# Attention and routed experts on one core: a new order table for attention's 2230 tasks

## Chip, core and metric

One Trainium2 chip, one of its cores. The metric is the device time of one execution in microseconds (us). The kernel's five instruction streams are TensorE (PE, the matrix engine, with its weight loads shown apart as PEld), VectorE (DVE), ScalarE (ACT), GpSimd (POOL) and SyncE (SP), which here issues nearly all DMAs.

## What is computed

Attention over 8 batches of 12 heads (448 positions, head size 64) with RMS-normalized q and k, and behind it a router with 8 experts, each of which takes exactly 448 of the 3584 tokens:

```python
q_n, k_n = (rmsnorm(q, g_q), rmsnorm(k, g_k))
scores = np.matmul(q_n, k_n.transpose(0, 1, 3, 2)) / np.sqrt(64)
scores = scores - np.max(scores, axis=-1, keepdims=True)
attn = np.exp(scores)
attn = attn / (np.sum(attn, axis=-1, keepdims=True) + 1e-09)
x = np.matmul(attn, v).transpose(0, 2, 1, 3).reshape(3584, 768)
logits = x @ w_gate                       # (3584, 8)
# all 3584*8 logits are gone through from the largest down; a token goes to
# expert e if it has none yet and e has fewer than 448 tokens
out[mask_e] = np.maximum(x[mask_e] @ w1[e], 0.0) @ w2[e]
```

## The kernel before

The kernel has two stages. In the first, some 405 us long, attention makes the rows x and the logits; then the router assigns tokens, and the experts gather their rows and multiply. The change lies in the first stage alone.

**Tiling.** The 96 heads are 24 groups of four (`g`), each two pairs of heads; there are 48 pairs. For a group, q and k are loaded by SP (`_load` L242 for the first 384 positions, `_tails` L249 for the last 64), squared and summed (DVE L320), normalized (POOL L353), split into a high and a low f16 part (ACT L388, POOL, DVE), and turned by DMA transposes from SP (L429). Then a first product on PE gives score maxima (`max_score` L539, DVE's `max_reduce` L550 reads them from the PSUM tiles `pm` and `psc`). The maxima of a group become one row of the second operand: ACT's `put_max` L555, PE's transposition (L485), ACT's copy `mt` (L489) and SP's two small DMAs `q<-mt` (`row_max`, L496). After that PE computes `scores` (L569, into `psc`), ACT exponentiates (`exp`, L580) and PE multiplies by the values (`av`, L604, f32, accumulated in the bank `po`; for part of the pairs the last 64 positions come apart, in 64-row matmuls, `av_tail`). DVE divides by the sum (`x_norm`, L639 to L643), ACT and DVE split x into f16 parts (`x_hi` L654 and L655, `x_lo` L660 and L661), PE transposes a part of it (`x_here`, L678, into the pair's own `po` bank), DVE copies it out (`x_here_out`, L371), DMAs turn the rest (L691) and store it (L700, L704), and PE multiplies by the gate's weights (`gate` L741 to L750; for the last batch `gate_last` L762 to L764). The logits of a batch come out as a sum (`gate_lo` on ACT, L783 and L784, then `gate_sum` on DVE, L789 and L790), of the last batch as a copy (`gate_copy`, L777 and L778).

**Buffers.** PSUM has two `psc` tiles, one `pm` tile and two `po` banks. The `po` banks carry the value products of a pair from its first `av` to its `x_here_out`, the gate's sums, and a few small things; so the value products of pair n+2 can't begin before pair n is done with. q and k have rings of two to three groups, the exponentials `e` one of nine tiles.

**Side work.** The router's constants are made in between: DVE casts the rank tables (`rankt`, `rankb`, both at L1143) and the second half of the gate's weights is made by `gate_weights` (L187).

**What sets the order.** `Attention.plan` lists 2230 tasks (763 on PE, 516 on DVE, 483 on ACT, 258 on SP, 210 on POOL), each with the tasks that it must follow. `Attention.ORDER`, a string of digit pairs in base 64, is a permutation of them. `Plan.run` (L84) decodes it and calls the tasks one after the other:

```python
order = [64 * digit[a] + digit[b] for a, b in zip(table[::2], table[1::2])]
assert all(a == b or at[a] < at[b] for a, b in self.edges())
for n in order:
    self.tasks[n][3](*self.tasks[n][4])
```

Each engine executes its own instructions strictly in this order; between engines only semaphores hold it. So the table sets, on each engine, which task stands behind which. How far one task stands behind another on PE is given below in PE's work between the two: the number of matmuls that stand there, by the start-to-start times of their kinds in the trace.

Of the kernel before, what the change touches and what calls it, by code (L numbers as in the profile page):

```python
# [89 lines left out]
class Attention:  # L90
# [926 lines left out]
    def plan_first(self, plan, g, a, t):  # L1017
# [42 lines left out]
                 port=False, frees=[("rf", *x)])  # L1060

    ORDER = (
        "020z0o01080706000509030+0-100A0p0q0r04111213141u1t1v1w1x1y2n2r2p2o0w2q2s0x0y3G3F0s0B151T161U1718191V1A1B1C1D"
        "1W1X1E1F1Y1Z1K1G1a1H1J1L1M1NCi1c1b1+1-1i1j1z2L1ICj1kCkCmCo2M20212N2O2P1l221d231O242Q1m2t1e251fCpClCn261h272R"
        "1P2v1Q1R2C1r281g2u2S1SCq29G+H02T2U2D2V2wG-2W2xH1Cr0C2ACsCuCw2ECtH2CxCv2y2a2b2z2+2B2-3H2G1nH32X2Y1o1q2F1pH43I"
        "CyH6Cz0t3J2Z3KH52cC+D0ME303132H73h3m3k493j3i1s3l4A2k3n33MKH8MGH93L3p3M343N3P3O35373QC-2dD1D2MJD3D42HHAMF2IHB"
        "2e2JD53q2KD6D8MH36D73oD9HC2jHDHEHFML3r4B0uDADB3RMIS44CS5S6MNHGMOMPHHS73s2f3T3S3U3t3u3v2l3E2m4b4g4f4c3V3W4d4e"
        "543X3w38DCMRMMDD2gS82iDE2hS9MQDFDHHIHKHJHL4DDGSASBDIDJDKHODLDMSCSD3D4E3x39MSHMMY3AMVMWMUMXHNSE3B3CHP4h3z4j4F"
        "4G3y3+4H4I4J533e3-40410vSFSGDNSHDODPMZMaDQMbMTHQDSDRSISJSKHSHRHTMdDTMcHUDVDUHWDWSLSMDXHVHXHYHZ3ZSNMfMeSORU3a"
        "HaMgMjMmMlMh4L3bHbSPSQ4iSR4kSSST4M4KDYHcMiMkSUDZDaDb3Y3d554lHd4m574N5V3c4O5+4P5X5Y3f0D4n4p4o5W4RSV4q3g4Q485a"  # L1070
        "5z5Z56RVMnHeMoDdDcHgSWSXSYHfHhSZDeDfSaDgMqMpHiMrMtSbDhMsHjScDiHkRW4344Hl0E0F450GSdSeSfSgSh58MuHmHnMxHoMwMzHq"
        "MvSu4r4s42HpHrDj46SmSl4vSvDkDlRXN0MyDmN2N4M+DoHsHuN1DnSwSxSy595b4t5A4u475B5D5CHtHv4x5EDpDrSzM-S+Dq5cHwN3HyN5"
        "HxHzS-DsT0H+5dH-Dt4TRYI0I24UN8N9NB5FT1T2T3T4T5I14VI3Sn4w5eT6T75-4X5H5f5g61DuDvDw5G4S5I5h5i4ySj4Y6P6u4W6U5J6R"
        "4Z6Q5K4aNANCRZDxNFN6NGNEDyDzD+NHN7I4E06ST8T90HD-62TAI6NISk6t6T525L5j5kI5I7I8I9E1E2IANJNDTBICIB4zIDTCTFTGTHTI"
        "4+TDIEIF4-IGTE0ITJSoSqTKSp60TLE3Sr50IH636451Ss5l6V5n6XE4StE5Si655m5o665pNKNLNONNNQRaE6NMNPIIE86768IKIJILNWNR"
        "IM6WTMTNTOE7TPTQIONSINIP6YTRE9TSEANVNXNTNUEBRbECTTTUTVED6Z696a6v6xIQIRTWISNYNZNb5r6b6A5M5q5S7J7O7n5NIT5O5PIU"
        "IV6B5R6c6C6d5Q6yTXTkTlEE6wEFEGRcNgNkNcNeEHNiNaIWEJEINdTmTnToIYIXIZTd7o7K7L6DTp6f6g6F6e5s5T6E7N7M5U5yEKEMNfNj"
        "IaIcNhIbIdIeIfELTqTrTsENEONlIgRd5t5uIh5v6zTtTuTvTwTxNoIiNpNsNmNqIj0J6h7P6+7R5x6i6-70TyTzEPEQERReNxNnES5wNzIk"
        "NvEUETImNrT+T-U0IlIoInIpU173EVEWEXU2NuNyIqNwEYIsIrIt6jTbTcNtEZU3IuU5U6U7U46H6k71746l726G6IIwTeTfTgU86J7QU9UA"
        "0K0LUB7STZTa6M8D6KIvIxThEaEb7p6L7T7UN+O3N-O0Ti0M757V767X7Y7W778i6N6O8H78TY8F8E8I8G79Ec7rEdO1O2TjEfEe7sIyI+Iz"  # L1080
        "I-O4RfJ0EgO7O8UCUDUEEiJ1UFUGEhJ2J4J3J57ZO5O6EjUHO9J6OAOBEk0NUI7qRgUJUK6nJ76o6p7bOGULElJ87t7uUM7aJ9EmUNEnODOF"
        "OHOEOIUaEo7c6r6m6q7A7v7w7x8J8LUbEpRhOJOCEqErEtUcEsONJAOPJCJBJD8h6s7d7f7y7e7GUS97JEEuJGOMOOOLOKUdUeUfEvUgUhUi"
        "8KJFJH7B7C7z0O7DJIJKRiJJJM0P8MUjUkUl0QJLJN8j7-8N8OUm7FEwEx0REy7EUTUR7+808P8Q8R81838S7g82997H989b7IUOOUOROVOQ"
        "OTEzOSOWJOE-JQ0SJPJRUqUrUnUsE+UoJSUpJUUtJTJV8kUuUUUWUVUvF0UwF1OXOYUXF3F2F48TOcOZOaObUY8l8m7hUZ7i7jJW8nJX8oF5"
        "F6F79DRjJYOhOjOdJaJZOfOeF8OgOi8p8U8VUx0TUyUz9EFA7kJb7lU+8W8q8r8s9C9A9BUQ9c8X8YJcJeJdOkJgJfJhF9U-V0V1FBRkFCFD"
        "V2V3V4Ji9FJj8tV5OrFEOqOmOoFF85JkOpOlV686V7On87JlV8RlV9VAVB9GJmJoOtOuOwOvOs7mUP9dA1848u8ZJnVCJp9H8a0U8v9I9f89"
        "VD9eVQVRFGOyOxRmFHFIFJP0O+FLVSVTVU88JqP2A68xA3A2A48A8w8B8yJsFK9J9K9L9M8zJrVVJtVJA5AV8CVHO-JuP3JwJvJxA7VW9gVX"
        "VYFMRnJyOzP1FNFOVZ0VVaVbJz9NFPFQP8P7J+K0Vc9h8bJ-8cVdPAP5VeVf8d9iK19O9PFRFSFTA80WA98fRoPBPHPDPCFUP4P9P68eK2FW"
        "VgFVVhVi9R9j9k9Q9l9n9mK40XK3K5VjPGFXFZPEK6K7K8PFKAFYVkVnVoVp9T9o8+K9KBFaVlKCFbVmKEVI9SAWAx8gBQVq8-90VKVrVsVL"
        "VMAAVtKD91KFFcPIPLPNPOVNPJPKABAC9pAXAZVO92ADAE9rAH93FdFeAYVPPMFfRpPSKGAaFhVuFgVvVw0Y9qAFAGAIAbAcAd9tKHKIKJVx"  # L1090
        "PPPTKKKL0ZAe0a9UFiPRPUVyFjKMFkFlVzPVV+PQFmKOKNRq9V9WKP9XKQPYPcKSPaV-W0W1W2W3WGWHKRKTAzVFVG949sAyB1AJVEFn9YA+"
        "A-9596B0AL0bAKAh0cAfAi0d0e0fAgANFoFpPWPbPZPXFqRrFsWIWJWKFrKUPhKWPePfPjKVWLKXFt9ZWMWNFuWOKYKZB39uFvPiFwRsPdKa"
        "FxKb9vPgKcKdWPWQWRWSPmKe9wKgPqPlKf9xKhB2WTB4B5B6AjWUWVAMBPW89aW7BRBT9z9yAlBrW9FyFz0gF+RtPkPoF-G0PuPvPnPrG1G2"
        "PpG4WWWXG3BSWYAkKiKjB7B8BBB9BCAnBAAOPsPxKkKmG5PtKlKnKoPwWZKqG6KpAPKr0hWaAQWbKsWdWeWf0iWcARWgWhBUKuKtKvWAWCWi"
        "WBAmBvBsBuBt9+BwASCKG7WDBVWEBDBWBxBzWjG8PyQ2WFG9GARuP+Q9PzGBGCGDGFBEBFBXBYBZAoBHGEQ3KwQ1KyKxKzGGK+P-BbK-0j0k"
        "B+GHQ0WkWlWmByL0ApQ6L1AqL2ArWnWoQ4L4Q5Q8L3L5BG9-A0WpGIQ7L6ATW4AsCJW5W6WqGJGKRvQCQGWr0lWsWtGLBaBcL7B-C0BdWuBf"
        "AUC1BeC2BIBhGMWvGNQEQAL8QFQBQDX6GOBgX7RwGQGPX8X90mXAL9LACLCNQHLCLBLDGRLEGSXBLFBJLGQLQJBKXCXDCOCMXELIQIQKBLLH"
        "AtQMLKLJCPLLRxGT0nGUQNQTQQQSGWQPXFGVXGXHW-W+BMAuAvWzBOAwC3C4C7C8CAC5C6C9GYLMXICQCRCSLNXJGXQOQRLOQULQXMXNXOXK"
        "XLLPLRXPGZGaXQX0LSX3X1XRX2GcGbLTX4BNXSX5LUGdQVQYBjBkRyLVBlLWQXQWLYQaQbQZCTCUBiCVCXCYLXLZBmWxLaCBLcLbLdYrQcQe"
        "GeXTXUXVXWGfXXGgQdQfLeQgQhQiXYLfBnXZGhRzGjGiXaXbXcLgLiQmLhLjGkQlQkQjLkGlGmGnGoLlXdQpLmQnCDCECFQoLnCaCWBoCZCb"  # L1100
        "CCCcWwBpBqCGWyXeXfXgGpGqGrR+QuQsGsQqQrGuXhXiXjLoQtLqQvCHLpXkLsLrLtQwGtXlXyXzGvR-GwLuLvX+GxX-Y0Y1QxQzGyLwLyQy"
        "Q+GzY2LxCdCeCfS0L+CIXpXoCgXrLzL-R0Q-R3R1R2R4R5M0ChM2R6R7Y6Y7Y8Y9YAM1M3M4M5M6S1M7M8R8M9RCMARARBR9YFYGYHYIYJMC"
        "RFRERDS2MBMDY3YNYOYPYQYRY4RLRKRMRHRIYKS3RORNRJRGRRRPRSRTRQYWYXYYYLYZYaYBYeYfYgYhYiYDYbYcYSYCXqYlYjYkYTXsXuXt"
        "XvXwXxYnY5YEYoYpYUYVYMXmXnYdYqYm"
    )

    def run(self):
# [933 lines left out]
```

## Time and profile before

| | |
|---|---|
| median of three runs | 902.78 us (902.22 to 904.13) |
| the profiled execution | 904.41 us, its span 902.6 us |
| mean granted clock of TensorE in it | 0.984 of full speed |
| PE busy | 863.4 us, 96% of the span |
| DVE, ACT, POOL busy | 628.0, 469.2, 401.6 us |
| the first router count (L1379) | starts at 406.3 us |

The span runs from the first to the last instruction. A busy PE is one with a matmul in its pipe; between 0 and 400 us its idle time stands in few waits, which the trace lists by line and by what ended them.

### The profile page before, as it was taken

How to read it: one execution, taken by the hardware profiler on the slowest of the kernel's cores; microseconds unless marked ns; L12 is line 12 of the kernel's file. 1: busy time of each engine (PE TensorE's matmuls, PEld its weight loads, DVE VectorE, ACT ScalarE, POOL GpSimd, SP SyncE). 2: the span in 40 equal slices, each digit the busy share in tenths (PEclk: the TensorE clock that was granted, in tenths of full speed). 3: DMA queues.
4: the chain of work that ended last, by engine and by line, in shares of the span. 5: the costliest groups of instructions: out<-in, count | busy, mean ns of one | idle time of the engine just before them, and what ended most of it. 6: DMA issues, size and time to landing. Idle time of an engine off the chain costs nothing.

```text
span 902.6 us, 27569 instructions
## 1 busy us (share of the span) xinstructions
PE 863.4 (96%) x11763; PEld 557.4 (62%) x11765; DVE 628.0 (70%) x1503; ACT 469.2 (52%) x739; POOL 401.6 (44%) x448
## 2 busy tenths in 40 slices
PE   5989999999999999995999999999999999999996
PEld 2467777677777777784556555565555655555553
DVE  6999888888888988737887776866768675143100
ACT  4987887688887786650434333333333333242110
POOL 7899999889998897202103021101111120200001
PEclk9999999999999999995999999999999999999998
DMA  7677999999899998424747096785929387591001
GB/s 187 145 176 150 195 194 190 207 191 203 193 197 203 174 211 136 118 49 140 259 153 258 28 280 184 207 231 168 278 67 303 114 251 222 169 246 39 27 18 44
DMA packets 253019, 153.64 MB, mean 170 GB/s; under 512 B 178654, under 2 KB 240094, under 8 KB 251872
## 3 DMA queue, kind: packets, MB, share of 16 engines
q1 hardware_dynamic: 247388, 129.39, 60.8%
q0 software_dynamic: 4704, 22.03, 7.3%
q8 instruction: 92, 1.51, 0.7%
q10 hardware_dynamic: 804, 0.46, 0.2%
q14 instruction: 31, 0.25, 0.1%
HBM read 94.43 MB, written 22.02 MB: 129 GB/s over the span
## 4 chain that ended last, share of the span: by engine, by line
PE 66%; issue 18%; DVE 5%; POOL 3%; DMA 3%; ACT 2%; SPq 1%; POOLq 0%; DVEq 0%; ACTq 0%
PE po L604 15%; PE ph L1804 15%; PE py L1821 13%; PE psc L569 12%; PE pm L539 2%; PE py L1830 2%; PE psc L539 1%; DMA qkraw<-in_q_dram 1%; POOL out_dram L1840 1%; DVE mx L550 1%; POOL rows L1737 1%; PE rp L1450 1%; DMA q<-mt 1%; PE pm L536 1%; SPq L249 1%
## 5 line engine op out<-in xcount | busy, mean ns | idle before, releaser
L1804 PE MATMUL ph<-xt,w1h 128*128 128x448 f16 (+2 forms) x804 | 209.5, 344 | 0.0
L604 PEld LDWEIGHTS po<-v,e 128*64 128x64 f32 (+1 forms) x5376 | 172.1, 138 | 41.2 <-issue 20.2
L604 PE MATMUL po<-v,e 128*64 128x65 f32 (+1 forms) x5376 | 185.8, 224 | 2.7 <-DVE xt L371 1.5
L580 ACT ACTIVATE e<-psc 128x896 f32<-128x896 f32 x168 | 151.1, 916 | 57.3 <-PE psc L569 55.8
L1840 POOL DMA_INDIRECT out_dram<-y,idx x32 | 34.3, 1073 | 280.1 <-ACT y L1823 245.7
L569 PE MATMUL psc<-q,k 128*64 128x448 f16 x1344 | 153.5, 354 | 2.1 <-POOL st L333 0.9
L1804 PE MATMUL ph<-xt,w1l 128*128 128x448 f16 (+2 forms) x402 | 135.1, 344 | 0.0
L1821 PE MATMUL py<-w2h,hl 128*128 128x384 f16 x384 | 125.0, 326 | 0.0
L1821 PE MATMUL py<-w2l,hh 128*128 128x384 f16 x384 | 125.0, 326 | 0.0
L1821 PE MATMUL py<-w2h,hh 128*128 128x384 f16 x384 | 125.0, 326 | 0.0
L1804 PEld LDWEIGHTS <-w1h 128*128 128x128 f16 x804 | 74.0, 97 | 63.8 <-issue 2.3
L550 DVE TENSOR_REDUCE mx<-pm 128x2 f32<-128x896 f32 x96 | 104.2, 1085 | 8.4 <-PE pm L539 6.0
L1792 ACT ACTIVATE hh<-ph 128x448 f16<-128x448 f32 x64 | 34.8, 543 | 144.4 <-PE ph L1804 139.6
L1821 PEld LDWEIGHTS <-hh 128*128 128x128 f16 x768 | 73.3, 97 | 46.4
L569 PEld LDWEIGHTS <-k 128*64 128x64 f16 x1344 | 73.6, 110 | 36.8 <-issue 7.5
L1823 ACT ACTIVATE y<-py 128x384 f32<-128x384 f32 x48 | 23.5, 490 | 132.6 <-PE py L1821 104.2
L1737 POOL DMA_INDIRECT rows<-xd,idx x32 | 31.8, 995 | 127.4 <-DVE idx L1631 43.2
L550 DVE TENSOR_REDUCE mx<-psc 128x2 f32<-128x896 f32 (+1 forms) x74 | 77.8, 1058 | 6.5 <-PE psc L539 5.7
L1794 DVE SCALAR_TENSOR_TENSOR hl<-ph,hh 128x448 f16<-128x448 f32 x64 | 39.2, 619 | 60.4 <-ACT hh L1792 60.2
L1724 DVE SCALAR_TENSOR_TENSOR w2l<-stage,w2h 128x768 f16<-128x768 f32 x64 | 60.1, 950 | 22.2 <-ACT w2h L1720 22.1
L1724 DVE SCALAR_TENSOR_TENSOR w1l<-stage,w1h 128x768 f16<-128x768 f32 x64 | 59.4, 950 | 3.3 <-ACT w1h L1720 3.3
L1720 ACT ACTIVATE w1h<-stage 128x1536 f16<-128x1536 f32 x32 | 47.2, 1476 | 21.4 <-DMA stage<-in_moe_w_dram 21.4
(294 smaller groups left out, 1425.3 us busy)
## 6 DMA issues: line engine op xcount, KB each, us to landing
stage<-in_moe_w_dram SPq DMA_DIRECT2D x64, 768.0 KB
vraw<-in_v_dram SPq DMA_DIRECT2D x24, 384.0 KB
xd<-xb SPq DMA_DIRECT2D x8, 1152.0 KB
qkraw<-in_q_dram SPq DMA_DIRECT2D x23, 384.0 KB
qkraw<-in_k_dram SPq DMA_DIRECT2D x23, 384.0 KB
vraw<-in_v_dram SPq DMA_DIRECT2D x24, 64.0 KB
xd<-xm SPq DMA_DIRECT2D x16, 96.0 KB
qkraw<-in_k_dram SPq DMA_DIRECT2D x22, 64.0 KB
```

The source lines that it names most:

```text
L550: self.nc.vector.tensor_reduce(m, p[:, :k, :448], axis=AX.X, op=OP.max)
L569: nc.tensor.matmul(p[64 * h:64 * h + 64, i, :448], kt[:, a, n + 64 * h:n + 64 * h + 64], qt[:, a, 448 * s:448 * s + 448], start=st, stop=n ...
L580: self.nc.scalar.activation(e, p[:, :, :448], AF.Exp, scale=scale)
L604: self.nc.tensor.matmul(self.po(pair)[64 * n:64 * n + 64, w], self.T["e", d][r, i, q:q + 64], self.v1[g % 2][r, self.slot(a, u, s)], start ...
L1720: self.nc.scalar.activation(h, v, AF.Copy, scale=self.WS)
L1724: self.later(0.93, lambda w=w: self.nc.vector.scalar_tensor_tensor(l[:, w], v[:, w], self.WS, h[:, w], op0=OP.mult, op1=OP.subtract), k, i)
L1737: nc.gpsimd.indirect_dma_start(out=g[:n, c, :], out_offset=None, in_=self.xd, in_offset=bass.IndirectOffsetOnAxis(ap=idx[:n, c:c + 1], axi ...
L1792: nc.scalar.activation(hh, whole, AF.Relu)
L1794: self.later(0.6, lambda: nc.vector.scalar_tensor_tensor(hl, whole, 0.0, hh, op0=OP.max, op1=OP.subtract), k, 3.5, f)
L1804: nc.tensor.matmul(p, a[:, i, c], x[:, b, o], start=j == 0, stop=j == 17)
L1821: nc.tensor.matmul(p, a[:, f, s], b[:, f, o], start=st, stop=sp)
L1840: st = nc.gpsimd.indirect_dma_start(out=self.out, out_offset=bass.IndirectOffsetOnAxis(ap=self.router.idx[k][:n, c:c + 1], axis=0), in_=y[ ...
```

## The change

Only `Attention.ORDER` is different. The tasks, their number, engines, costs, buffers and dependencies are the same, and so is everything behind attention. Of the tasks, 660 on PE, 374 on DVE, 383 on ACT, 139 on POOL and 215 on SP stand at another place of their engine's row; by 3.4, 2.4, 2.5, 1.6 and 3.5 places in the mean. The first line of the table, before and now:

```diff
@@ -1060,48 +1060,48 @@
     ORDER = (
-        "020z0o01080706000509030+0-100A0p0q0r04111213141u1t1v1w1x1y2n2r2p2o0w2q2s0x0y3G3F0s0B151T161U1718191V1A1B1C1D"
...
+        "0z11020+120o0-13011008071u0600051t090A030p0q14161v0r04151w1U0B181x171T191y1V1A2n1B1W1C2r1D1E2p1X1F2o1Y1G1Z1K"
...
```

Three places, each on DVE. The first is the cast of the rank tables. Before, both casts (128 x 224 and one row of 8) stand between the split of pair 15's x (L660, L661) and the copy of its transposed part (L371):

```order
L643 TENSOR_TENSOR po<-po,z 128x7x64
L371 COPY xt<-po 128x2x128
L320 TENSOR_REDUCE st<-sq_133 128x14
L660 TENSOR_TENSOR xb<-po,xb 128x2x3x64
L661 TENSOR_TENSOR xm<-po,xm 128x64
L1143 CAST rankt<-rank 128x224
L1143 CAST rankb<-rank 1x8
L371 COPY xt<-po 128x2x128
L320 TENSOR_REDUCE st<-sq_134 128x14
```

Now the casts stand earlier and apart. The first stands ahead of the split of pair 13, the second ahead of that of pair 14; at pair 15 the copy follows the split at once:

```order
L643 TENSOR_TENSOR po<-po,z 128x7x64
L1143 CAST rankt<-rank 128x224
L660 TENSOR_TENSOR xb<-po,xb 128x2x3x64
L661 TENSOR_TENSOR xm<-po,xm 128x64
...
L643 TENSOR_TENSOR po<-po,z 128x7x64
L1143 CAST rankb<-rank 1x8
L550 TENSOR_REDUCE mx<-pm 128x2
L660 TENSOR_TENSOR xb<-po,xb 128x2x3x64
L661 TENSOR_TENSOR xm<-po,xm 128x64
```

The second is `gate_weights`, around the splits of pairs 0 and 1. Before, it stands between the division of pair 1's rows (L643) and their split:

```order
L641 RECIPROCAL z<-z 128x7
L643 TENSOR_TENSOR po<-po,z 128x7x64
L320 TENSOR_REDUCE st<-sq_134 128x14
L187 SCALAR_TENSOR_TENSOR wg<-wg_123,wg 128x18x8
L660 TENSOR_TENSOR xb<-po,xb 128x2x3x64
L661 TENSOR_TENSOR xm<-po,xm 128x64
L371 COPY xt<-po 128x2x128
```

Now it stands behind that split, and ahead of the copy of the same pair's transposed part; three of the maxima have come ahead of the split:

```order
L641 RECIPROCAL z<-z 128x7
L643 TENSOR_TENSOR po<-po,z 128x7x64
L550 TENSOR_REDUCE mx<-pm 128x2
L550 TENSOR_REDUCE mx<-psc 128x2
L550 TENSOR_REDUCE mx<-pm 128x2
L660 TENSOR_TENSOR xb<-po,xb 128x2x3x64
L661 TENSOR_TENSOR xm<-po,xm 128x64
L187 SCALAR_TENSOR_TENSOR wg<-wg_123,wg 128x18x8
L371 COPY xt<-po 128x2x128
```

The third is the end of attention, the last rows ahead of the router. Before, batch 6's sum of logits (L789, L790) comes ahead of two copies of transposed rows (L730), and batch 7's copy of logits is last:

```order
L643 TENSOR_TENSOR po<-po,z 128x7x64
L660 TENSOR_TENSOR xb<-po,xb 128x2x3x64
L661 TENSOR_TENSOR xm<-po,xm 128x64
L730 COPY xt<-psc 128x6x128
L789 TENSOR_TENSOR logits<-po,lsc 128x24
L790 TENSOR_TENSOR logits<-po,lsc 64x8
L730 COPY xt<-psc 128x6x128
L730 COPY xt<-psc 128x2x128
L777 COPY logits<-po 128x24
L778 COPY logits<-po 64x8
```

Now batch 6's sum is last; on PE three of the four parts of batch 6's gate have moved behind all of batch 7's:

```order
L643 TENSOR_TENSOR po<-po,z 128x7x64
L730 COPY xt<-psc 128x6x128
L660 TENSOR_TENSOR xb<-po,xb 128x2x3x64
L661 TENSOR_TENSOR xm<-po,xm 128x64
L730 COPY xt<-psc 128x6x128
L730 COPY xt<-psc 128x2x128
L777 COPY logits<-po 128x24
L778 COPY logits<-po 64x8
L789 TENSOR_TENSOR logits<-po,lsc 128x24
L790 TENSOR_TENSOR logits<-po,lsc 64x8
```

## Rows read from the trace of the kernel before

**Rows 1.** Busy time of each engine over the span, from the page.
```profile
PE 863.4 (96%) x11763; PEld 557.4 (62%) x11765; DVE 628.0 (70%) x1503; ACT 469.2 (52%) x739; POOL 401.6 (44%) x448
```
**Rows 2.** Stretches: start:end, length, busy us by engine, granted clock, DMA share, GB/s.
```profile
20.00:80.00 60.00, 54.62 (x861) 34.82 (x861) 55.30 (x85) 51.95 (x87) 54.80 (x53) 1.00 0.71 154
80.00:160.00 80.00, 78.45 (x1713) 56.81 (x1709) 68.69 (x116) 63.96 (x111) 75.05 (x75) 1.00 0.99 193
160.00:180.00 20.00, 18.63 (x385) 14.12 (x383) 17.62 (x30) 14.55 (x26) 16.71 (x16) 0.91 1.01 196
180.00:400.00 220.00, 218.00 (x4955) 165.31 (x4950) 177.83 (x327) 167.74 (x289) 167.23 (x163) 1.00 0.85 170
```
**Rows 3.** PE's waits, 0 to 410 us: us in total, times, longest.
```profile
PE po L678 <- DVE xm L661: 2.0, 1, 2.0
PE po L604 <- DVE xt L371: 1.5, 2, 1.3
...
PE po L604 <- issue: 1.1, 1, 1.1
...
PE psc L569 <- POOL st L333: 0.9, 1, 0.9
...
PE pm L539 <- POOL k L397: 0.3, 1, 0.3
...
PE psc L569 <- DMA q<-mt: 0.2, 1, 0.2
```
**Rows 4.** PE's timeline, 396 to 400 us: start, us, line, matmuls, tile shape.
```profile
395.80 4.01 PE L604 MATMUL po<-v,e 64*64 64x65 f32 x124
399.75 0.51 PE L715 MATMUL psc<-ident,xb 128*128 128x128 f16 x6
```
**Rows 5.** PE's timeline, 169 to 175 us; in brackets idle time before and its releaser.
```profile
171.20 3.26 PE L604 MATMUL po<-v,e 128*64 128x65 f32 x60 [1.28 <-DVE xt L371]
174.40 0.36 PE L539 MATMUL pm<-k,q 64*128 64x448 f16 x2
174.60 0.35 PE L539 MATMUL psc<-k,q 64*128 64x448 f16 x2
174.88 0.34 PE L604 MATMUL po<-v,e 128*64 128x65 f32 x4
```
**Rows 6.** DVE's timeline, 166 to 173 us: start, us, line and operation.
```profile
168.64 1.51 DVE L1143 CAST rankt<-rank 128x224 bf16<-128x224 f32 x1
170.07 0.88 DVE L1143 CAST rankb<-rank 1x8 bf16<-1x8 f32 x1
170.88 0.27 DVE L371 COPY xt<-po 128x256 f16<-128x256 f16 x1
```
**Rows 7.** DVE's timeline, 396 to 407 us.
```profile
399.44 0.56 DVE L660 TENSOR_TENSOR xb<-po,xb 128x384 f16<-128x384 f32 x1 [0.73 <-ACT xm L655]
406.11 0.17 DVE L778 COPY logits<-po 64x8 f32<-64x8 f32 x1
```
**Rows 8.** PE's timeline, 354 to 356 us.
```profile
354.29 0.36 PE L539 MATMUL pm<-k,q 64*128 64x448 f16 x1
354.98 0.35 PE L539 MATMUL pm<-k,q 64*128 64x448 f16 x1 [0.32 <-POOL k L397]
```
**Rows 9.** DVE's timeline, 58 to 66 us.
```profile
62.37 2.17 DVE L187 SCALAR_TENSOR_TENSOR wg<-wg,wg 128x144 f16<-128x144 f32 x1
65.85 1.09 DVE L550 TENSOR_REDUCE mx<-pm 128x2 f32<-128x896 f32 x1
```
**Rows 10.** ACT's exponential (L580), all of them: durations min/median/max in ns.
```profile
L580 ACT ACTIVATE e<-psc x168: 889/917/967, 28.7 to 391.1; 128x896 f32<-128x896 f32 x168
```
**Rows 11.** PE's timeline around the scores at 158.6 us.
```profile
158.63 0.76 PE L569 MATMUL psc<-q,k 128*64 128x448 f16 x6 [0.89 <-POOL st L333]
```
**Rows 12.** ACT's timeline, 396 to 407 us.
```profile
403.40 0.19 ACT L784 ACTIVATE lsc<-po 64x8 f32<-64x8 f32 x1
```
**Rows 13.** SP's timeline, 150 to 160 us.
```profile
153.26 1.68 SPq L496 DMA_DIRECT2D q<-mt  x2
```

## What the change does to the time: the prediction

> **What bounds the kernel now.** I read the busy times first: PE is at work for 863.4 of 902.6 us [rows 1], so a change that moves tasks and removes none can only win what PE idles, or what its matmuls take beyond their steady rate. Next the stretches [rows 2], since attention ends at 406 us and all that changes lies before. Of the 380 us from 20 to 400, PE is busy for 54.62 + 78.45 + 18.63 + 218.00 = 369.7 us; 10.3 us are idle, 5.4 of them before 80. The clock stands at 1.00 but for 0.91 between 160 and 180. Then the waits by line [rows 3], which say where the idle time sits: 2.0 us once before a transposition (L678), 1.3 us once before a value product (L604), 1.1 us that nothing in the program released, 0.9 and 0.2 us before scores, 0.3 us before maxima. These named waits are the ceiling of what a better order can take back; the other engines are below 75% over the span and matter only where PE stands still for them.
>
> **Part by part.** Places are compared in the order of each engine; distances on PE are in PE's work, with 32 ns for a value product (124 of them from 395.80 to 399.75 [rows 4]) and 0.10 us for a 448-wide matmul (two from 174.40 to 174.60 [rows 5]).
>
> *The rank casts.* At 168.64 DVE starts 1.51 us of rankt, then 0.88 us of rankb, and only at 170.88 the copy of pair 15's transposed part [rows 6]. The next value products need the bank that this copy frees, and PE waits 1.28 us for it [rows 5]. In the new order the copy stands right behind the split. It then waits only for PE's transposition (on PE, 0.3 us from about 168.8) and ends near 169.4, while PE arrives at 171.20 - 1.28 = 169.92. Margin 0.5 us: the wait goes, **-1.28** (bounds -1.28 and 0). Where the casts went they cost DVE 1.43 us (168.64 to 170.07) ahead of pair 13's split; there DVE waits for ACT's half anyway, some 0.7 us as in the one row that shows it at a quiet place [rows 7]. The remaining 0.7 us hit a transposition with more than 3 us of PE work before the bank is needed, so I take nothing (bound +0.7).
>
> *The clock behind that wait.* The 60 value products from 171.20 to 174.40 took 3.20 us [rows 5]; at 32 ns they take 1.9. That is the lower of the two clock levels (1.2 against 2.4 GHz), the cause of the 0.91 in that stretch [rows 2]. The row puts the fall right behind the 1.28-us wait, so I take **-1.3** with the wait (bounds 0, and -1.8, which is 0.09 of 20 us). Against this stands that the 2.0-us wait at 65 us [rows 3] left its whole stretch at 1.00 [rows 2]: a single wait does not bring the fall each time. The Trainium skill ("TensorE: Matmul & The Clock Gate", What's actually happening) says that the gate opens and closes by how busy the array has been lately. By that rule the fall belongs to the load around it and may come at any other wait; the sum would then be 1.3 higher. The trace has one case for the row and one for the rule.
>
> *Weight shapes.* PE's order now changes between the three tile shapes (64 x 128, 128 x 64, and the 64 x 64 of the parts that come apart) 257 times, 271 before. A change costs what two matmuls ahead of one take more than two ahead of their like: from 174.60 to 174.88 0.28 us, against 0.20 from 174.40 to 174.60 [rows 5]: 0.08 us. Fourteen of them are 1.1 us; by the kinds that go (more of the dearer f32 ones) I take **-1.4** (bounds -1.1, -1.7).
>
> *The late copy of k at 354 us.* The second of two matmuls began at 354.98, 0.69 us behind the first, where 0.10 is usual, because POOL's duplicate of k (L397) came late [rows 8]. In the new order it has 5.8 us of PE work more or less to spare: **-0.5** (bounds -0.6, 0).
>
> *The wait that nothing released,* 1.1 us at 266.9 [rows 3]. One packet of instructions was fetched then, behind full DMA engines. Whether it meets the transfers again depends on shifts that I can't foresee: half of it, **-0.5** (bounds -1.1, 0).
>
> *gate_weights* (2.17 us on DVE [rows 9]). It no longer stands ahead of pair 1's split, the cause of PE's 2.0-us wait. But it now stands ahead of pair 1's copy, and ahead of pair 0's split DVE has 2.6 us more to do (maxima of 1.09 us each [rows 9]) where PE comes only 0.9 us later, so a new wait of some 1.6 us arises there. Net 0 (bounds -1.0, +1.6).
>
> *Exponentials.* ACT needs 0.92 us [rows 10] between a score product and the values that use it. Distances under 2 us of PE work: 2 before (least 1.57, and no wait there), 11 now (least 1.07). If ACT is free at once, only the shortest two or three wait, +0.4 together; if it is in the middle of another exponential each waits some 0.3 more, +3. I take **+1.5**.
>
> *Accumulators.* A score tile is used again within 1.5 us in 41 places instead of 64, a maxima tile within 1.2 us in 10 instead of 4, against 1.09 us of DVE for the maxima: 0 (bounds -0.6, +0.6).
>
> *The row of maxima.* From the transposition of a group's maxima to its first scores stand 4 to 8 us of PE work. Two waits show what the small DMA chain needs: 0.9 us in group 8, whose distance was 5.5, and 0.2 in group 5, distance 6.2 [rows 3, 11], so 6.4 at those places (the first row names POOL's L333, which was long done; what came last is the small DMA issued from 153.26 on [rows 13], 5.4 us before the matmul); other groups did with 3.5 to 5. Under 6.4 there were 16 groups of 22, and are 16 now, but other ones: groups 2, 5, 15, 18 and 19 lose 0.4 to 2.1 us, groups 7, 8, 9 and 14 win. **+0.3** (bounds -1.1, +5.4, below).
>
> *The end.* The last logits went from PE through one DVE copy to the count. Now they go through ACT (L784, 0.19 us [rows 12]) and then a DVE sum of the copy's length [rows 7], so +0.3. Batch 7's gate now comes ahead of one transposition and asks for a bank that pair 47's split frees, about 0.5 us later than PE gets there: **+0.8** in all (bounds +0.3, +1.0).
>
> Sum: -1.28 - 1.3 - 1.4 - 0.5 - 0.5 + 1.5 + 0.3 + 0.8 = **-2.4** against the profiled execution's 904.4, so 902.0. The median of the runs, 902.78, is 1.6 below that execution; so **900.4**.
>
> **The rivals.** (a) *Rows of maxima land late; slower.* SP issues the two small DMAs (1.68 us for the pair [rows 13]) between loads and transposes; the DMA engines are 99% and 85% busy over 80 to 160 and 180 to 400 [rows 2]. If every group needs the 6.4 us, groups 5, 15, 18 and 19 wait 1.6 + 0.8 + 0.7 + 1.1, group 2 (which did without a wait at 4.8, and has 3.65) 1.2: 5.4 us, and one clock fall of 1.3, against 1.1 that goes. The sum becomes -2.4 - 0.3 - 1.1 + 5.4 + 1.3 = +2.9, 905.7. It decides once these waits pass some 4 us together. For it: two waits of the kind in the trace. Against: 14 short groups showed none, and in group 5 fewer loads stand ahead. The Trainium skill ("DMA: Bandwidth & Descriptors", Queues, rings and completion order) has descriptors consumed in ring order on each DMA engine, so that a row waits for whatever was issued ahead of it; no row here shows it apart. Chance 0.18.
> (b) *Waits only change places.* With gate_weights at +1.6 and the clock's fall at another wait (+1.3), the sum is -2.4 + 2.9 = +0.5: 903.3, no change. For it: DVE is 92% busy from 20 to 80 us [rows 2] and gets no less work. Chance 0.24.
> (c) *The clock alone stays*: -1.1, 901.7; also no change. Chance 0.10.
> (d) *Everything goes*: the clock never falls, no exponential is late (+0.4), the fetch is hidden (-1.1): -2.4 - 1.1 - 0.6 = -4.1, and with -1.0 at gate_weights and no late rows (-1.4) -6.5: 896.3. It shares the forecast's side.
>
> **How the numbers follow.** A measurement of this kernel can tell about 0.2%, 1.8 us. The forecast and (d), together 0.48, are faster; of (b) and (c) a small part is too: faster 0.52. No change 0.29 from (b), (c) and the forecast's upper end. Slower 0.19, from (a) and a sliver of (b). The range goes from (d) at 896 to (a)'s lower half at 905. The likeliest case's own range is 897.5 to 901.5.
>
> **What would show it.** Right: no wait at L604 for L371 near 170 us, 1.00 in the stretch 160 to 180, no wait for L397 near 355, L1379 beginning near 404. Wrong: several waits of PE at L569 for `mt` or at its releasers, a granted clock under 1.00 in a stretch between 20 and 400, more than 2 us of PE's waits at L604 for ACT's L580, or a wait at L678 for L661 of 2 us or more.

## The result, and the profile after

The changed kernel takes **913.01 us** in the median of 7 runs (909.35 to 914.38), the kernel before 904.35 in 7 runs (902.22 to 907.71): a ratio of 1.0089, 95% interval 1.007 to 1.0108. It is slower, by 8 us; the prediction was 900.4, its range 896 to 905. The profiled execution of the new kernel took 914.38 (span 912.6). The first router count (L1379) begins at 416.24 us where it began at 406.33: nearly all that was lost, 9.9 us in these two executions, lies in attention.

The stretches of the kernel after, in the columns of [rows 2]:

```profile
20.00:80.00 60.00, 56.63 (x914) 35.91 (x914) 56.37 (x87) 52.43 (x87) 56.28 (x56) 1.00 0.75 159
80.00:160.00 80.00, 75.53 (x1625) 55.84 (x1619) 65.92 (x114) 60.10 (x105) 70.13 (x71) 0.98 0.97 187
160.00:180.00 20.00, 20.00 (x459) 16.50 (x457) 17.39 (x33) 17.23 (x31) 18.73 (x17) 1.00 0.88 204
180.00:400.00 220.00, 209.20 (x4638) 158.47 (x4638) 179.53 (x313) 160.46 (x277) 167.09 (x164) 0.98 0.91 174
```

Up to 80 us PE gained 2.0 us of busy time, and from 160 to 180 another 1.4 with the clock at 1.00. From 80 to 160 it lost 2.9, from 180 to 400 8.8. Finer stretches of the same view show where most of it went: one at 140, one at 280, and three in a row from 320 on.

```profile
140.00:160.00 20.00, 16.64 (x319) 11.76 (x319) 13.22 (x23) 12.78 (x22) 13.50 (x17) 0.91 0.97 189
...
280.00:300.00 20.00, 18.16 (x389) 13.72 (x387) 16.55 (x28) 13.95 (x23) 17.97 (x17) 1.00 1.08 176
...
320.00:340.00 20.00, 17.65 (x379) 12.72 (x377) 18.71 (x33) 13.22 (x22) 18.02 (x18) 0.96 0.91 195
340.00:360.00 20.00, 17.79 (x417) 14.30 (x413) 17.31 (x32) 11.70 (x20) 15.72 (x14) 0.96 0.59 145
360.00:380.00 20.00, 17.55 (x339) 11.86 (x341) 15.37 (x27) 11.00 (x18) 7.40 (x7) 0.91 0.45 74
```

PE's timeline has four long waits there, the last of them from 357.79 on, across two stretches; in brackets stand the wait and its releaser, as in [rows 5]. The first row is that of the weight load (PEld) ahead of the first wait:

```profile
143.25 0.33 PEld L569 LDWEIGHTS <-k 128*64 128x64 f16 x6 [4.14 <-DMA q<-mt]
143.26 0.94 PE L569 MATMUL psc<-q,k 128*64 128x448 f16 x6 [3.87 <-POOL st L333]
...
282.54 0.76 PE L569 MATMUL psc<-q,k 128*64 128x448 f16 x6 [1.84 <-DMA q<-mt]
...
336.94 0.36 PE L539 MATMUL pm<-k,q 64*128 64x448 f16 x2 [2.35 <-DMA q<-qs]
...
362.45 0.42 PE L678 MATMUL po<-ident,xb 128*64 128x128 f16 x4 [4.66 <-DVE xm L661]
```

The four make 12.7 us. The first is a wait for the row of maxima of group 7: the weight load names the DMA (4.14 us for q<-mt), POOL's L333 only signalled last. The second is for that of group 16. Of the waits of before [rows 3] none over 0.2 us is left. Summed over attention, without one wait of 7.5 us at its start that both kernels have, PE idles 20.6 us, 12.1 before: 8.45 more. The clock, 1.00 in the other stretches between 20 and 400 us, lost 0.09 + 0.04 + 0.04 + 0.09 of 20 us, 5.2 us, where it had lost 1.8: 3.4 more. Together that is 11.85 us more, but only 9.9 were lost, so the rest became some 1.9 us shorter.

**The fourth wait** is the costly one, and the prediction did not speak of what caused it. DVE's timeline ahead of it, in the kernel after: the task `early`, the router's first preparation (L1250 to L1260, then L1290), runs as one block behind batch 5's logits and ahead of pair 39's division, and the split that PE waits for (L661) stands behind it.

```profile
351.33 0.33 DVE L1250 TENSOR_REDUCE best<-logits 128x21 f32<-128x168 f32 x1
351.69 1.53 DVE L1251 TENSOR_TENSOR score<-logits,best 128x168 bf16<-128x168 f32 x1
353.14 0.86 DVE L1255 TENSOR_SCALAR keyi<-best 128x21 int32<-128x21 int32 x1
...
354.07 0.91 DVE L1256 TENSOR_TENSOR keyi<-best,keyi 128x21 int32<-128x21 int32 x1
...
355.25 1.91 DVE L1257 TENSOR_SCALAR keyi<-keyi 128x21 int32<-128x21 int32 x1
...
357.23 1.85 DVE L1258 TENSOR_SCALAR keyi<-keyi 128x21 int32<-128x21 int32 x1
...
359.20 0.85 DVE L1290 TENSOR_TENSOR cmp<-key,hit 128x672 bf16<-128x672 f32 x1
...
362.18 0.21 DVE L661 TENSOR_TENSOR xm<-po,xm 128x64 f16<-128x64 f32 x1
```

The same block in the kernel before:

```profile
347.39 0.33 DVE L1250 TENSOR_REDUCE best<-logits 128x21 f32<-128x168 f32 x1
...
349.27 0.17 DVE L1256 TENSOR_TENSOR keyi<-best,keyi 128x21 int32<-128x21 int32 x1
...
349.76 0.17 DVE L1257 TENSOR_SCALAR keyi<-keyi 128x21 int32<-128x21 int32 x1
...
350.05 0.17 DVE L1258 TENSOR_SCALAR keyi<-keyi 128x21 int32<-128x21 int32 x1
...
350.34 0.85 DVE L1290 TENSOR_TENSOR cmp<-key,hit 128x672 bf16<-128x672 f32 x1
```

It lasted 3.8 us (347.39 to 351.19) and lasts 8.7 now (351.33 to 360.06). Nothing in it changed, and in DVE's row it stands at the same place, with 457 tasks ahead of it, behind the same maxima and ahead of the same division. Single instructions on 21 numbers per partition went from 0.17 to 1.9 us. What differs is POOL. Its timeline, after:

```profile
353.03 1.91 POOL L397 COPY k<-k 64x896 f16<-64x896 f16 x2
355.03 2.09 POOL L378 TENSOR_TENSOR qn<-qn,gg 128x896 f32<-128x896 f32 x1
357.07 1.98 POOL L417 TENSOR_TENSOR ks<-kn,ks 128x896 f16<-128x896 f32 x1
```

and before, with the idle 1.36 us in which the quick instructions of the block ran:

```profile
347.25 1.91 POOL L397 COPY q<-q 64x896 f16<-64x896 f16 x2
350.52 2.42 POOL L422 TENSOR_TENSOR qs<-qn,qs 128x896 f16<-128x896 f32 x1 [1.36 <-ACT qs L388]
```

After, L1257 ends at 357.16 and POOL's L378 at 357.12; L1258 ends at 359.08 and POOL's L417 at 359.05. Each of these small instructions ends where a POOL instruction ends. POOL's row says why it was busy: before, its split of q (L422) stood right behind that copy of q and waited for ACT; in the new order a normalization, a copy of k, a gain and a split of k stand between the two, and the wait for ACT, 7.19 us long, comes at 359.05, behind the slow part of the block. It works the other way round too: the 2.42 us of L422 before fell beside DVE's L1290, and the same instruction takes 1.89 in the median.

### The profile page after: what moved, and what is told of

It is laid out like the page before. It is cut to its first block, busy times and chain, and to the rows that moved or that the text cites. A ratio compares the mean times of both kernels' runs of the same rounds, so it can differ in the third digit from the quotient of the medians.

```text
span 912.6 us, 27589 instructions
## 1 busy us (share of the span) xinstructions
PE 866.6 (95%) x11765; PEld 562.3 (62%) x11765; DVE 632.2 (69%) x1503; ACT 467.9 (51%) x739; POOL 400.1 (44%) x448
## 3 DMA queue, kind: packets, MB, share of 16 engines
q8 instruction: 92, 1.51, 0.7%
## 4 chain that ended last, share of the span: by engine, by line
PE 55%; issue 19%; POOL 9%; DVE 7%; DMA 5%; ACT 2%; SPq 1%; POOLq 0%; ACTq 0%; DVEq 0%
PE ph L1804 15%; PE py L1821 13%; PE po L604 10%; PE psc L569 8%; DVE mx L550 2%; PE py L1830 2%; DMA k<-ks 1%; PE pm L539 1%; POOL qs L422 1%; POOL out_dram L1840 1%; POOL q L397 1%; DMA qkraw<-in_q_dram 1%; POOL rows L1737 1%; PE rp L1450 1%; PE psc L539 1%
## 5 line engine op out<-in xcount | busy, mean ns | idle before, releaser
L604 PEld LDWEIGHTS po<-v,e 128*64 128x64 f32 (+1 forms) x5376 | 173.2, 138 | 37.1 <-issue 20.1
L604 PE MATMUL po<-v,e 128*64 128x65 f32 (+1 forms) x5376 | 187.3, 224 | 0.2 <-DVE xt L371 0.2
L580 ACT ACTIVATE e<-psc 128x896 f32<-128x896 f32 x168 | 151.1, 914 | 54.3 <-PE psc L569 52.2
L569 PE MATMUL psc<-q,k 128*64 128x448 f16 x1344 | 158.0, 358 | 7.1 <-POOL st L333 3.9
L569 PEld LDWEIGHTS <-k 128*64 128x64 f16 x1344 | 77.1, 111 | 37.9 <-issue 9.2
L550 DVE TENSOR_REDUCE mx<-psc 128x2 f32<-128x896 f32 x74 | 78.0, 1058 | 4.1 <-PE psc L539 3.8
```

What stands on the lines that cost most here:

```text
L550: self.nc.vector.tensor_reduce(m, p[:, :k, :448], axis=AX.X, op=OP.max)
L569: nc.tensor.matmul(p[64 * h:64 * h + 64, i, :448], kt[:, a, n + 64 * h:n + 64 * h + 64], qt[:, a, 448 * s:448 * s + 448], start=st, stop=n ...
L580: self.nc.scalar.activation(e, p[:, :, :448], AF.Exp, scale=scale)
L604: self.nc.tensor.matmul(self.po(pair)[64 * n:64 * n + 64, w], self.T["e", d][r, i, q:q + 64], self.v1[g % 2][r, self.slot(a, u, s)], start ...
```

## Experiments

Twelve kernels, each timed beside the kernel before on the same chip. Edits of the table are shown as rows of the queue concerned, by task names.

| | median us | ratio to before, 95% interval |
|---|---|---|
| the change itself | 913.01 | 1.0089 (1.007 to 1.0108) |
| 1: group 7's row first on SP | 910.88 | 1.0086 (1.0067 to 1.0104) |
| 2: block late on DVE | 902.31 | 1.0001 (0.9977 to 1.0025) |
| 3: both, and two more on SP | 904.40 | 1.001 (0.9995 to 1.0024) |
| 9: block late, six moves on SP | 905.56 | 1.0015 (1.0001 to 1.0029) |
| 10: block behind pair 39's copy | 908.57 | 1.0056 (1.003 to 1.0082) |
| 11: block late, x turned later | 903.73 | 1.0006 (0.9986 to 1.0025) |
| 7: POOL's order of before | 939.97 | 1.0395 (1.0358 to 1.0432) |
| 4: casts, on before | 902.80 | 0.9992 (0.9975 to 1.0009) |
| 5: gate_weights, on before | 902.75 | 0.999 (0.9971 to 1.0009) |
| 6: POOL's gap filled, on before | 904.49 | 0.9996 (0.9976 to 1.0016) |
| 12: block late, on before | 902.56 | 0.999 (0.9968 to 1.0012) |
| 8: casts, gate_weights, block, on before | 900.24 | 0.9949 (0.9926 to 0.9972) |

**1. Group 7's row of maxima first.** SP's timeline after shows what stood ahead of it. ACT had written `mt` at 132.63; SP came to the two small DMAs at 136.70, behind a transpose whose issue lasted 4.82 us, a store of 1.15 MB (L700), and four loads, issued from 132.57 on:

```profile
127.03 4.82 SPq L429 DMA_TRANSPOSE q<-qs  x1
131.90 0.57 SPq L700 DMA_DIRECT2D xd<-xb  x1
...
134.37 1.48 SPq L242 DMA_DIRECT2D vraw<-in_v_dram  x1
135.89 0.71 SPq L249 DMA_DIRECT2D qkraw<-in_k_dram  x1
136.70 1.65 SPq L496 DMA_DIRECT2D q<-mt  x2
```

```diff
 tr_q1[8]
+row_max[7]
 x_store[0,0]
 load_qk[12,0]
 load_qk[12,2]
 load_v[8,0]
 load_qk[12,4]
-row_max[7]
 x_dma_turn[1,1]
```

> The new order, with group 7's two small DMAs of maxima ahead of the store of 1.15 MB and the four loads that stood before them on SP; nothing else moves. Theory A (the waits are places that add up): PE's 3.87 us wait at 143 us goes nearly whole, and with it the clock's fall there (0.91 of one 20-us stretch, 1.8 us): about 908 from 913. Theory B (POOL, busy 19 of each 20 us, is the second bound and hands what is saved to the next wait): the wait at 143 goes, but those at 282, 337 and 362 stay or grow, and the time falls by 2 at most, about 911 to 913.

Theory B by its time: the ratio is that of the change. The wait at 143 went, those at 282 and 337 became 0.82 and 1.66, and the one at pair 39 stayed, 4.69. But ten microseconds behind the first PE now waits for the transposed q of group 9, which the theory did not name:

```profile
153.14 0.36 PE L539 MATMUL pm<-k,q 64*128 64x448 f16 x2 [3.06 <-DMA q<-qs]
```

**2. The block late.**

```diff
 max_reduce[155]
-early
 x_norm[39,0]
...
 x_lo[42]
+early
 x_norm[43,0]
```

> The new order, with the router's first preparation (the task early, lines 1250 to 1260 and 1290, one block on DVE) moved from ahead of pair 39's division to behind pair 42's split, when POOL has nothing left to do. Theory A: the block lasts 8.7 us because its small integer operations run beside POOL; at its new place it lasts under 4, PE's wait of 4.66 at 362 goes, with the clock's fall behind it (1.8): about 907 from 913. Theory B: POOL is late by then and the same wait comes back at the next pair as a wait for POOL or its transposes; the block still shortens, the time falls by 2 at most. If the block lasts as long at its new place, POOL has nothing to do with it.

Theory A, and more than its price of 6 us: the loss is gone, 0.88% between the two ratios, 8 us. The block lasts 2.94 us at its new place, behind POOL's last instruction, and the integer instruction of 1.91 us is back at 0.17:

```profile
374.98 0.32 DVE L1250 TENSOR_REDUCE best<-logits 128x21 f32<-128x168 f32 x1
...
376.50 0.17 DVE L1257 TENSOR_SCALAR keyi<-keyi 128x21 int32<-128x21 int32 x1
...
377.07 0.85 DVE L1290 TENSOR_TENSOR cmp<-key,hit 128x672 bf16<-128x672 f32 x1
```

From 331 us to the router PE has no wait over 0.3 us, and the clock from 340 to 400 is 1.00. The wait itself (4.66) and the falls from 340 to 380 in the change (0.04 and 0.09 of 20 us, 2.6) make 7.3 of the 8. Other waits differ between the two profiles as well; the last section comes back to them.

**3. Both, and two more moves on SP.**

```diff
 (1 and 2, and)
+tr_q1[21]
 x_dma_turn[5,2]
-tr_q1[21]
...
+row_max[16]
 load_qk[20,4]
 load_qk[20,3]
-row_max[16]
```

> The new order with four moves: the two above, group 16's small DMAs ahead of two loads, and group 21's transpose of q ahead of one transpose of x on SP. Theory A: the waits of 3.87, 1.84, 2.35 and 4.66 us and the falls of the clock behind them go: 12.7 and about 5, that is about 896 to 900. Theory B: half of it at most, 905 to 908.

Nearest to theory B: 904.4 is no better than the block alone. The waits at 337 and 362 are gone, and at 282 PE waits 0.65 us for an exponential and no more for a row, but the wait that left 143 is at 152.64, 3.01 us for POOL's copy of k, which had waited for k's transpose.

**9 and 11. More of SP's order.** Both have the block late (2) and group 21's transpose of q early (3); 9 has group 16's small DMAs early too. In 9 the transposes of x of batch 1 stand behind group 9's transposes, in 11 behind group 8's small DMAs, where the order before has them.

```diff
 tr_q1[8]
+row_max[7]
 x_store[0,0]
...
-x_dma_turn[1,1]
-x_dma_turn[1,2]
 tr_k1[9]
 load_qk[12,1]
 tr_q1[9]
+x_dma_turn[1,1]    (9)
+x_dma_turn[1,2]    (9)
...
 row_max[8]
+x_dma_turn[1,1]    (11)
+x_dma_turn[1,2]    (11)
```

> The new order with the preparation block late, and six moves on SP: group 7's small DMAs of maxima ahead of the store and loads; two transposes of x behind group 9's transposes of k and q (they stood ahead of them, and with the small DMAs first PE waited 3.0 us for group 9 at 153); group 21's transpose of q ahead of a transpose of x; group 16's small DMAs ahead of two loads. Theory A: the waits of some 2.3 (140 to 142) and 1.8 (331), with its fall of the clock (1.8), go and none comes: 902.3 less 4 to 6, about 897 to 898. Theory B: a transposed k or row of maxima is late at another place and 1 to 3 us come back: 900 to 902.

> The new order with the block late, and on SP: group 7's small DMAs first, both transposes of x of batch 1 behind group 8's small DMAs (where the order before has them, near 157 us, instead of 138), group 21's transpose of q ahead of a transpose of x. Theory (between 125 and 160 us the new order put a store of 1.15 MB and two transposes of x, 3 us each, among the rows and transposes that PE needs next; whichever stands behind them comes 3 to 4 us late): no wait of PE over 1 us between 125 and 165, 902.3 less 2.3 and less the wait of 1.8 at 331, about 898 to 899. Rival (the DMA engines are simply full there, and something is late in any order): a wait of 2 to 4 us at another group, 902 to 906.

In 9 what theory B says came, a late row elsewhere, at more than its price (905.56 where it had 900 to 902). In 11 the rival holds. The wait moves from group to group: 3.81 us for group 8's row in 9; in 11 1.16 for that row and 2.14 for group 10's transposed q.

```profile
159.36 1.13 PE L569 MATMUL psc<-q,k 128*64 128x448 f16 x8 [3.81 <-DMA q<-mt]
```

```profile
157.16 1.14 PE L569 MATMUL psc<-q,k 128*64 128x448 f16 x10 [1.16 <-DMA q<-mt]
...
168.87 0.36 PE L539 MATMUL pm<-k,q 64*128 64x448 f16 x2 [2.14 <-DMA q<-qs]
```

So 2 to 4 us of waiting between 125 and 170 came with every order of SP that was tried, and do not belong to one place of it. Which part of the new order brings them (the loads, POOL's order, PE's being earlier) stays open.

**10. The block six places later only.**

```diff
-early
 x_norm[39,0]
...
 x_here_out[39]
+early
 max_reduce[156]
```

> The new order with the preparation block moved six places of DVE's row only: behind pair 39's division, split and copy, still in the time in which POOL works. Theory (PE waited because the block stood ahead of a split that PE asked for 6.5 us after the block began, with room for 4 us of it): PE's wait at pair 39 goes, the block still lasts over 5 us beside POOL, and what follows it (two reads of maxima, then pair 40's division) is late by less: about 904 to 907 from 913. Rival (only its length beside POOL counts, wherever it stands): 910 to 913.

Between the two. The wait at pair 39 went, but the maxima behind the block are late instead. The block lasted 4.97 us: its integer instructions met an idle POOL and took 0.16 to 0.18, while L1290, a two-input instruction, met the next POOL instruction and took 2.56 instead of 0.85:

```profile
355.28 0.17 DVE L1259 CAST key<-keyi 128x21 f32<-128x21 int32 x1
...
355.49 2.56 DVE L1290 TENSOR_TENSOR cmp<-key,hit 128x672 bf16<-128x672 f32 x1
```

```profile
355.46 1.88 POOL L422 TENSOR_TENSOR qs<-qn,qs 128x896 f16<-128x896 f32 x1 [1.48 <-ACT qs L388]
```

```profile
359.11 0.36 PE L539 MATMUL pm<-k,q 64*128 64x448 f16 x2 [3.00 <-DVE mx L550]
```

**6. POOL's gap filled, in the kernel before.** One POOL instruction is added whose result nobody reads; DVE's row is untouched.

```diff
             if e == "P":
                 self.nc.gpsimd.tensor_copy(o, i)
+                if (name, g, p) == ("q1", 21, 1):
+                    self.nc.gpsimd.tensor_tensor(self.fill, self.T["q1", g][:, 0], self.T["q1", g][:, 1], op=OP.add)
```

> The order before, and one more POOL instruction, an addition of two halves of q into a tile that nobody reads, some 1.9 us, behind the duplicate of q of group 21; it fills the 1.4 us at 349.2 in which POOL stood idle while DVE ran the router's first preparation. The table is that of before. Theory (DVE's small integer instructions wait for whatever POOL instruction runs beside them): the block, 3.8 us before, becomes some 2 us longer or more, though no DVE instruction has moved. The copy of k at 355 comes 0.5 us later and PE's wait there grows from 0.3 to 0.8. Rival (its length follows from its place in the order or from its data): 3.8 us as before. Time: 0 to 3 us more.

The theory. The block takes 7.54 us instead of 3.80 (lines are three higher in this kernel). POOL, then DVE:

```profile
350.89 1.94 POOL L400 TENSOR_TENSOR fill<-q 128x896 f16<-128x896 f16 x1
352.79 1.99 POOL L425 TENSOR_TENSOR qs<-qn,qs 128x896 f16<-128x896 f32 x1
```

```profile
349.03 0.33 DVE L1253 TENSOR_REDUCE best<-logits 128x21 f32<-128x168 f32 x1
...
351.39 1.47 DVE L1260 TENSOR_SCALAR keyi<-keyi 128x21 int32<-128x21 int32 x1
...
352.94 1.87 DVE L1261 TENSOR_SCALAR keyi<-keyi 128x21 int32<-128x21 int32 x1
...
355.72 0.84 DVE L1293 TENSOR_TENSOR cmp<-key,hit 128x672 bf16<-128x672 f32 x1
```

PE's wait for the copy of k grew from 0.32 to 1.13 us, but the time did not rise by anything that can be measured, and that is the second half of the explanation. In the order before, pair 39's transposition comes 10.6 us behind the block's start (347.39 to 358.00), and division and split need 2.4 of that (359.97 to 362.39 in the change), so a block of 7.5 us still fits:

```profile
358.00 0.28 PE L678 MATMUL po<-ident,xb 128*64 128x128 f16 x4
```

In the new order this transposition stands seven tasks earlier in PE's row, and PE asks for it at 357.79 (362.45 - 4.66), 6.5 us behind the block's start: 4.1 us of room, and 8.7 - 4.1 is, within 0.1, the wait of 4.66. So it took both, a block that lasts longer and a transposition that comes sooner; the 3.8 us of before would have fitted in 4.1. That last step is worked out from the rows: no run has the new order with a short block at its old place. **12**, the kernel before with the block late, agrees that the block cost nothing there:

```diff
-early
 x_norm[39,0]
...
 x_lo[43]
+early
 x_norm[44,0]
```

> The order before, with the preparation block alone moved to behind pair 43's split. Its 3.8 us stood in 10.6 us of PE's work there, so it should have cost nothing: within 1 of the kernel before, and the gain of the kernel with three moves belongs to the casts and gate_weights. If the time falls by 2 or more, the block did cost time in the order before.

902.56, no difference that can be measured.

**7. POOL's order of before in the new order.**

```diff
 dup_k[8]
+rsqrt[10,3]
 lo_k[9]
 dup_q[7]
-dup_q[8]
...
```

> The new order on PE, DVE, ACT and SP, with POOL's order of before. Theory C (the new order of POOL made it late, so that the preparation block met a busy POOL and the transpose of q at 337 came late): the block lasts under 5 us, the waits of 2.35 and 4.66 go, about 903 from 913. Theory D (POOL's own order is not the cause, the lateness comes from the SP and DMA chain behind 140 us): within 3 of 913, the block still over 7 us.

Both theories fall: 940 us. PE waits for POOL 14 times, 25 us in all, in four places 4.2 to 4.9 us:

```profile
149.94 1.33 PE L569 MATMUL psc<-q,k 128*64 128x448 f16 x6 [4.79 <-POOL q L397]
```

The orders of the engines are made for one another, and a run with one of them exchanged says nothing about what that one did in the change. What it does show is how little room POOL has.

**4 and 5. The casts and gate_weights alone, in the kernel before.**

```diff
 x_norm[13,2]
+rankt
 x_lo[13]
...
 x_norm[14,2]
+rankb
...
 x_lo[15]
-rankt
-rankb
 x_here_out[15]
```

> The order before, with the two casts of the rank tables alone moved to where the new order has them. By the prediction PE's wait of 1.28 at 171 goes with the clock's fall behind it: 2.6 less, about 900 to 902 where the kernel before has 902.8 to 904.4. If the casts cost DVE more beside POOL there, or the fall comes elsewhere, nothing is gained (within 1).

```diff
 sumsq[5,1]
-gate_weights
 x_lo[1]
+gate_weights
 x_here_out[1]
```

> The order before, with gate_weights alone behind pair 1's split instead of ahead of it. By the row of before, PE's wait of 2.0 us at 65 goes. Theory A (places add up): about 901.3 from 903.3. Theory B (POOL and the DMA chain behind it set the pace, so PE meets the next wait): within 1 of 903.3. The instruction itself lasted 2.17 us there and 0.53 in the new order; if POOL's instruction beside it decides, it lasts anything from 0.5 to 2.2 here.

Neither is a difference that can be measured. In 4 the wait at 171 went, but the cast, moved without the ACT step that makes its input, waited 1.58 us for it, and PE 1.52 behind that; the new order moves the ACT step as well. In 5 the wait of 2.0 became 0.89, since gate_weights took 1.56 us ahead of the copy.

**8. The three places together, in the kernel before.** Rows of 4, 5 and 12, and on ACT

```diff
 exp[50]
+rank
...
 exp[55]
-rank
 hi_q[10]
```

> The order before with three places of the new one: the rank table's ACT step 19 us earlier and both casts as in the new order (so that the cast doesn't wait for ACT, as it did with the casts moved alone), gate_weights behind pair 1's split, and the preparation block behind pair 43's split, when POOL is done. Theory A: the waits of 2.0 and 1.28 us and the fall of the clock go: 903.3 less 2.0 + 1.3 + 1.3 = 898.7. Theory B: half of that or less comes through, 901 to 903.

Between the theories, and the best kernel of the case: 0.9949, better than both orders. The waits for the copies are 0.93 and none; one of 2.02 for a row of maxima came at 204.8, with a fall of the clock to 0.91 behind it. Waits of this kind, at most 0.9 us in the kernel before, came in 4 (1.89 at 251) and 12 (1.65 at 253) too. Which of the moves gives the 0.5% is not shown: each of the three alone came to 0.999, within its interval of 1, and the cast's ACT step was moved here only.

## Why the prediction was wrong

**The step that failed** is in its first part: that the other engines "are below 75% over the span and matter only where PE stands still for them". POOL is busy 91 and 94% of the stretches from 20 to 80 and 80 to 160 [rows 2], and in the change through nearly all of the block, to 359.05; and it matters by setting how long DVE's instructions last. From that step came two errors. Durations of DVE's instructions were taken over as properties of the instruction ("2.17 us on DVE" for gate_weights, 1.51 for rankt). And places were compared within each engine, so that only tasks that moved there were priced: the block, which kept its place in DVE's row, had no term at all, though POOL's tasks had moved beside it and PE's transposition had come nearer. It was the largest one: it lasted 8.7 us instead of 3.8, PE waited 4.66, and moving it alone (experiment 2) took back the 8 us. That POOL makes the block longer is shown by experiment 6, in which no instruction of DVE was moved.

Of its signs of being right three came (no wait at L604 near 170, 1.00 from 160 to 180, no wait for L397 near 355), and L1379 near 404 did not. Of its signs of being wrong three came: waits for rows of maxima, a granted clock under 1.00, and a wait at L678 for L661 of over 2 us, this one at another pair and for another reason than gate_weights, for which it was meant. And the base was low: 902.78 was the median of three runs, seven give 904.35, so 1.6 us of the distance to 900.4 are the base's.

Term by term:
- *Casts*, -1.28: right. No wait for L371 over 0.2 us is left.
- *The clock behind them*, -1.3: wrong. The stretch 160 to 180 came to 1.00, but the clock fell in four others, 3.4 us more in all. This agrees with what the prediction set beside the term from the Trainium skill ("TensorE: Matmul & The Clock Gate", What's actually happening), that the clock follows how busy TensorE has been lately, so that the fall may come at another wait. Experiment 5 shows that the wait alone does not bring it: the same wait of 1.27 us at the same copy, and the 60 value products behind it took 2.0 us (170.26 to 172.26), not 3.2 [rows 5].

```profile
170.26 1.97 PE L604 MATMUL po<-v,e 128*64 128x65 f32 x60 [1.27 <-DVE xt L371]
172.26 0.36 PE L539 MATMUL pm<-k,q 64*128 64x448 f16 x2
```

- *Weight shapes*, -1.4: the remainder of the account above is -1.9, which fits, but holds whatever else changed; the term was not measured by itself.
- *The copy of k*, -0.5, and *the unreleased wait*, -0.5: both are gone, the second whole (1.1).
- *gate_weights*, 0: it gave 2.0, twice its bound. The wait of 2.0 went and the expected new one of 1.6 did not come; the instruction lasted 0.54 us instead of 2.17.

```profile
61.42 0.54 DVE L187 SCALAR_TENSOR_TENSOR wg<-wg,wg 128x144 f16<-128x144 f32 x1
```

- *Exponentials*, +1.5: no value product (L604) waits for L580 at all, so overpriced by the whole 1.5. PE's waits for L580 at other lines fell, from 1.3 us in all (0.9 and 0.4) to 0.7 (0.5 and 0.2).
- *Row of maxima*, +0.3, and rival (a): the mechanism came true in this profile with 3.87 + 1.84 us, against 0.9 and 0.2 that went, +4.6, near its upper bound. But the groups named (2, 5, 15, 18, 19) did not wait, and group 7, whose distance had grown, did. What decided there is what SP issued ahead of the row, 4.1 us of it, as experiment 1 shows, and not the distance on PE. In group 16, whose distance is unchanged, SP came only 1.1 us behind `mt`; the cause of that wait is not shown. That (a) named the slower side is luck: experiments 3, 9 and 11 have 3 to 4 us of waits behind SP's DMAs between 125 and 170 us, but not the block, and lie within 0.15% of the kernel before.
- *The transposed q at 337*, 2.35 us, and *the block*, 4.66: no term. Experiments 3, 9 and 11 removed the first by one move on SP, without gain in time over experiment 2.
- *The end*, +0.8: the last wait grew from 0.46 to 0.72 us and 0.17 came for the bank, +0.4.

Experiments 2, 3, 9 and 11 all lack the block's wait and lie between 1.0001 and 1.0015: without it the new order is a kernel as fast as before, not 2.4 us faster. Rival (b), waits that only change places, describes that remainder; its price of no change was right, its place was not.

## What to carry to other kernels

When an order is changed, ask of every long task on a shared engine what will run beside it and who stands behind it, also of those that did not move. A duration in the trace belongs to an instruction and its neighbours; a small VectorE instruction that takes far longer than its like and ends where a GpSimd instruction ends (here within 0.05 us) has waited, and its row is no price. And a wait that leaves one place in a chain without room (here SP, the DMA engines and POOL) should be expected at the next, so price the chain, not the place.

## What was not expected of the hardware

Instructions of the same shape on the same data lasted very differently. The cast of one row of 8 numbers took 0.88 us before [rows 6], 0.62 after and 0.15 in experiment 4; that of rankt 1.51, 0.27 and 0.87; gate_weights 2.17 [rows 9], 0.54, and 1.56 in experiment 5; the integer step L1257 0.17 or 1.91. The Trainium skill ("SBUF — State Buffer", Who interferes with whom) has VectorE and GpSimd share a pair of ports that one of them holds for a whole instruction; a VectorE instruction in a two-port mode, or with two inputs from SBUF against a GpSimd instruction that reads SBUF, contends for it, and whichever comes second is fully blocked. The ends at 357.16 and 359.08, the 2.56 us of a two-input instruction in experiment 10, and POOL's 2.42 us beside L1290 agree with it; so do the reductions (L1250, 0.32 to 0.33 us in every run), of which the Trainium skill says there that on this chip they never contend. No run shows the port itself.

Up to the block at 351 us the orders of the change and of experiments 2 and 10 are the same, and yet their profiles differ there. In the change group 7's row cost one wait of 3.87 us and group 16's one of 1.84; in the others the scores of group 7 waited 0.99 + 1.33 and 1.27 + 1.31 us (the first part of each is put down to DVE's L639), and those of group 16 not at all. So waits of one order at the end of a chain of DMAs differed by 1 to 2 us between these executions; a single profile prices them no better than that.
